# Joining each group's values burst with the next group's scores burst on TensorE, the values in an idle pair of PSUM banks

## Chip, cores and metric

One core of one Trainium2 chip. The metric is device time in microseconds of one execution: the median of three runs.

## What is computed

Local attention in chunks of 64 tokens, then a two-layer network with a squared ReLU. 8 sequences of 576 tokens with 8 heads of 64 give 4608 tokens of width 512; the hidden width is 2048. All data are float32.

```python
scores = scale * np.matmul(q_c, k_c.transpose(0, 1, 2, 4, 3))
scores = scores - np.max(scores, axis=-1, keepdims=True)
attn = np.exp(scores)
attn = attn / (np.sum(attn, axis=-1, keepdims=True) + 1e-09)
out = np.matmul(attn, v_c)
...
h = x @ w_in
r = np.maximum(h, 0.0)
g = s * (r * r) + b
return (g @ w_out).astype(np.float32)
```

## The kernel before

**Tiling.** The tokens come in 36 tiles of 128. The first four (class First) are done in a plain way while the weights are converted and written back to DRAM in pieces (kept). The other 32 tiles make four blocks of 8 tiles, 1024 tokens each, numbered 1 to 4; block 1 is the class Second, blocks 2 to 4 are the class Block. Every float32 product is made of three float32r products: an operand is split into a high part (hi, made on ACT) and a low rest (lo, made on DVE), and high x high, high x low and low x high are summed in PSUM.

**A block's products.** Blocks use a seven-product scheme for a 2x2 matrix product (P1, P7, P6, P2, P5, P4, P3, in this order, the list SEQUENCE). Layer one ("up") has four chains pp = 0 to 3 of seven products, slots 0 to 27 of a block. Layer two ("down") is one chain whose seven products take four slots each, slots 28 to 55. One slot is one product: 12 wide matmuls (128x128 weights, 512 columns), L575 for up, L624 for down (these lines are of the kernel before; the changed one has them a line further down). The names p0 to p55 in the code are these slots. Block 1 has a slightly different start and therefore 57 slots.

**PSUM.** Eight banks in four pairs. One pair, the tile ps_a, belongs to attention (steady_bank, L423). The other three, ps_o (two of them) and ps, are a ring for the chains: a Chain takes the ring's order and reverses it for the next chain, P1, P7 and P2 each begin one of the three pairs, and the other four products add onto these (Chain.bank, L443). On the way ACT copies a pair out (keep, L448) and DVE forms a quarter of the result from a pair and a copy (add, L455: form11 and others in up, end00 and others in down). form12 (L593) and the last quarter are read by ACT.

**Attention of the next block.** While a block runs its products, the attention of the block after it is done in four groups of two token tiles. One group's steps: load_qk and load_v (SP queue); scores (L318: 32 products 64x64x64 on TensorE, each two matmul records, into ps_a); peak and sub on DVE, which read ps_a; exp on ACT; sum, norm (add, reciprocal, multiply) and turn (transposing 32x32 blocks, L368) on DVE; swap, eight transfers of 64 KB that complete the transpose from SBUF to SBUF (L377, SP queue); values (L384, 32 products into ps_a again); x_out on ACT (L418), which copies ps_a into the tile xf. From xf, POOL makes sums and differences (x_sums, L506), ACT the high parts (xh, L524) and DVE the low ones (xl, L530).

**What sets the order.** Nothing is scheduled by the machine: each block has a list self.pre[slot] of named steps to be issued before a slot's product, filled by plan_up, plan_down and plan_following, and the engines take their instructions in that order. `self.at(slot, ...)` appends to a slot's list; `self.pre[n + k][:0] = ...` puts steps at its front. In blocks 2 and 3 the scores of the four groups are issued in slots 3, 14, 25, 36 and their values in slots 13, 24, 35, 45 (GROUPS and END, L481). For block 1 and the part before it, a list written out by hand (ORDER, L26) replaces the plan; its names are "1:p45" for slot 45 of block 1, "2:values.3" for the values of group 3 of block 2. A second list, SLOTS (L91), says which of 45 SBUF places each new tile gets.

The weights of each product come from DRAM (stream, L545: tile st, six buffers, 512 KB each), issued on the SP queue five slots ahead. SP also carries the swaps and the loads and stores, in program order; an instruction that waits there holds what is behind it.

These steps come up below. gh and gl are the high part (L598, ACT) and the low part (L603, DVE) of the operand that one down product needs for one pp; they are issued four slots or more ahead of it. end00 (DVE, L456) reads the pair that P2, slots 40 to 43, has completed. less21 and t2 (L611) are subtractions on POOL in blocks 2 to 4.

Of the kernel before, what the change touches and what calls it, by code (L numbers as in the profile page):

```python
# [32 lines left out]
shift4 2:load_qk.0 more3 exp.0 load_v.3 more2 lo2 down0 relu2 sign4 sign3.1 copy2 add4 relu3 sum.0 down1 scale5 rest2
norm.0 hi3.0 add3.1 load6 hi4 up4 hi3.1 load7 tail5 keep0 lo3.0 transposes.0 shift5 copies.0 more4 lo4 copy3 values.0
relu4 sign5 down2 copy4 lo3.1 add5 tail6 rest3 rest4 scale6 up5 x_hi.0 shift6 load8 x_out.0 sign6 more5 scale7 x_lo.0
add6 down3 relu5 shift7 hi5 copy5 load9 scores.1 hi6 lo5 load_qk.2 tail7 up6 sign7 tail8 rest5 add7 more6 peak.1
scale8 up7 relu6 sub.1 load10 scale9 lo6 more7 keep1 hi7 down4 shift8 keep6 shift9 relu7 sign8 copy7 sign9 copy6 add8
down5 exp.1 rest6 rest7 scale10 sum.1 up9 lo7 hi8 load12 keep7 up8 tail10 norm.1 tail9 lo8 more9 add9 more8 down6
relu8 copy8 relu9 load11 rest8 keep3 shift10 transposes.1 copy9 sign10 down7 scale12 2:load_v.0 rest9 hi9 add10
copies.1 lo9 up10 tail12 load14 hi10 keep2 values.1 scale11 lo10 more10 x_hi.1 shift11 up11 sign11 tail11 x_lo.1  # L40
relu10 add11 more11 shift12 down8 x_out.1 relu11 load13 sign12 keep8 hi11 scores.2 copy11 add12 copy10 rest11 down9
peak.2 sub.2 load15 keep4 lo11 up13 exp.2 load_qk.3 scale14 rest10 sum.2 keep9 more13 hi12 up12 norm.2 scale13 tail14
keep5 more12 lo12 tail13 transposes.2 shift14 keep11 relu13 down10 shift13 sign13 copies.2 relu12 add13 values.2
copy12 rest12 down11 sign14 hi13 copy13 lo13 keep13 add14 x_hi.2 up15 rest13 scale15 keep10 x_lo.2 tail15 keep12 up14
shift15 hi14 more14 x_out.2 lo14 more15 relu14 sign15 scores.3 copy14 add15 relu15 rest14 down12 peak.3 copy15 sub.3
stream hi15 down13 rest15 exp.3 lo15 1:st9 1:st4 sum.3 keep14 down14 1:combine0.2 keep15 norm.3 1:combined_hi0.2
down15 1:combine0.3 last out0 transposes.3 1:combine0.5 copies.3 steady 1:p0 1:x_sums.0 1:combined_hi0.5
1:combined_hi0.3 1:keep_combined0.5.0 1:keep_combined0.2.0 values.3 2:load_v.1 1:combine0.6 1:p1 1:keep_combined0.3.0
1:combine0.4 1:combined_hi0.6 1:xh6.0 1:p2 x_hi.3 1:combined_lo0.3 1:relu11.0 x_lo.3 1:keep_combined0.3.1 1:p3
1:combined_lo0.2 x_out.3 1:combined_lo0.5 1:keep_combined0.2.1 out1 1:combined_hi0.4 1:x_sums.1 1:keep_combined0.5.1  # L50
2:scores.0 1:keep_combined0.6.0 1:xh2.1 1:p4 1:xh4.0 1:xh3.1 2:peak.0 1:relu21.0 2:sub.0 1:p5 1:combined_lo0.4 1:xh6.1
1:st5 1:xl2.1 1:keep_combined0.4.0 1:combine0.7 1:keep_combined0.4.1 1:p6 1:relu12.0 1:st7 1:combine1.0 1:xh4.1 1:p8
1:xh3.0 2:exp.0 1:xl6.0 1:combined_hi0.7 1:xl3.0 2:sum.0 1:p7 1:st6 1:keep0.1 1:xl3.1 1:st11 2:norm.0 1:p9 1:st8
1:relu22.0 1:combined_lo0.6 2:load_qk.1 1:xl6.1 1:xh2.0 2:turn.0 1:p11 1:keep3.1 1:xl2.0 2:swap.0.1 1:gh0.0 1:xl4.1
1:keep_combined0.7.0 1:combined_lo0.7 2:swap.0.3 1:p10 2:swap.0.7 1:combine1.1 2:swap.0.4 1:st13 2:swap.0.2 1:st14
1:p13 2:swap.0.0 1:keep2.1 1:xl4.0 2:swap.0.6 1:form11.1 1:combined_hi1.0 1:st12 2:swap.0.5 1:combine1.2
1:keep_combined0.6.1 1:p12 1:st10 1:keep_combined0.7.1 1:combined_hi1.2 1:form21.1 1:combined_hi1.1 1:p15 1:st17
1:combine1.3 1:square11.1 1:keep_combined1.2.0 1:combined_hi1.3 2:values.0 1:combined_lo1.1 1:st16 1:form22.1 1:p16
1:keep_combined1.1.1 2:x_out.0 1:combine1.4 1:p14 1:st18 1:keep3.2 1:keep_combined1.3.0 1:combined_lo1.2
1:combined_hi1.4 1:combine1.5 1:keep0.2 2:scores.1 1:st15 1:form12.1 1:p17 2:peak.1 1:combined_lo1.0 1:combine1.6  # L60
1:p18 1:keep_combined1.0.1 1:keep2.2 1:st22 1:keep_combined1.2.1 1:square22.1 1:keep_combined1.0.0 2:sub.1 1:p20
1:st20 1:form11.2 2:exp.1 1:square21.1 2:sum.1 1:p19 1:st19 1:combined_lo1.4 1:keep_combined1.1.0 1:combined_hi1.6
2:norm.1 1:combined_hi1.5 1:keep_combined1.6.0 1:p22 1:form22.2 2:turn.1 1:p21 1:form21.2 2:swap.1.6 1:st21 1:gl0.0
2:swap.1.1 1:square21.2 2:swap.1.0 1:p23 1:less11.0 2:swap.1.4 1:st25 1:keep0.3 1:combined_lo1.3 2:swap.1.5
1:keep_combined1.4.0 1:form12.2 1:combine1.7 2:swap.1.2 1:p24 1:st23 2:swap.1.3 1:gh0.1 2:swap.1.7 2:load_qk.2
1:keep3.3 1:gl0.1 1:p25 1:st24 1:keep2.3 1:less11.1 1:combined_hi1.7 1:st29 1:less12.1 1:square11.2 1:p26 1:st37
1:form11.3 1:gh3.1 1:t2.0 2:xh0.0 2:values.1 1:gl3.1 1:st26 1:gh1.0 1:keep_combined1.5.0 1:keep_combined1.3.1
1:less12.0 1:p27 2:x_out.1 1:square11.3 1:combined_lo1.5 1:form22.3 2:scores.2 1:st27 1:gh1.2 column_sums 1:gl1.0
1:p28 1:gh3.0 1:square22.2 1:combined_lo1.7 1:gl3.0 1:p29 1:st28 1:gh0.3 2:peak.2 2:xh1.0 1:combined_lo1.6 1:gh0.2
1:p30 1:gh5.0 1:form21.3 1:st30 1:keep_combined1.7.1 1:keep_combined1.5.1 1:gl0.2 1:keep_combined1.7.0  # L70
1:keep_combined1.4.1 1:t2.1 1:keep_combined1.6.1 1:p33 1:st33 2:sub.2 1:less11.2 2:exp.2 1:p34 1:form12.3 2:sum.2
2:norm.2 1:gh2.0 1:gh1.1 2:turn.2 1:square22.3 1:gl0.3 1:st31 1:st34 1:less12.2 biases 1:p31 1:p41 2:load_v.2
2:swap.2.3 1:gh3.2 1:less11.3 2:swap.2.5 1:gh4.1 2:swap.2.2 1:less12.3 1:p32 1:st32 1:gh2.1 1:gl3.2 2:swap.2.0 1:gh3.3
1:gl2.0 2:swap.2.1 1:gh4.3 1:p35 2:swap.2.7 1:gl1.2 1:keep0.down 2:swap.2.6 2:load_qk.3 1:gh5.1 1:gl2.1 2:swap.2.4
1:square21.3 1:p37 1:gl1.1 1:st38 2:st0 1:st39 1:gl3.3 1:t2.2 1:p38 1:st35 1:gl4.1 1:gh2.2 1:gh1.3 1:combine0.0 1:p36
1:st36 1:gh4.0 1:gl2.2 finish 1:t2.3 2:values.2 store 1:less21.1 1:p42 2:x_out.2 1:gl5.1 2:load_v.3 1:gh6.1 1:st40
1:combine0.1 2:xh0.1 1:gh2.3 2:scores.3 1:st42 2:xl0.1 1:p39 2:xl0.0 2:peak.3 1:gl2.3 1:p43 1:st41 2:sub.3 1:gl1.3
# [5 lines left out]
2:x_out.3 2:x_sums.1 1:combined_lo0.0 1:p51 1:st50 1:gl5.3 1:p52 1:st52 1:gl5.2 2:xh3.1 1:p53 1:st51
1:keep_combined0.0.1 1:end10 1:scaled10 2:x_sums.0 1:p54 2:xh2.1 2:xh6.1 1:scaled00 2:xl6.1 1:p55 2:st4 2:st1 2:xh3.0
2:xh2.0 2:xh4.0 1:p56 2:st2 2:xh5.1 2:xl4.0 1:scaled11 2:xl3.1 2:xl5.1 2:xh4.1 2:xl3.0 1:end01 2:st3 2:xl5.0 1:store10
2:xl2.0 3:load_v.0 2:xh6.0 2:xl1.1 2:xl1.0 1:store00 1:store11 2:xl2.1 2:xl6.0 2:xl4.1
"""

# [18 lines left out]
"""  # L107


@with_exitstack  # L110
def local_attention_then_squared_relu_mlp(ctx: ExitStack, tc, qkv, w, s, b, out):
# [10 lines left out]
    N = 2  # L122
# [959 lines left out]
```

## Time and profile before

| | |
|---|---|
| time, median of 3 runs | 775.91 us (775.17 to 779.9) |
| span of the profiled execution | 775.4 us; the page gives no other time of it |
| PE busy | 765.4 us, 99% of the span |
| DVE, ACT, POOL busy | 544.9, 489.4, 158.8 us |
| granted TensorE clock | full in all 40 slices |

How to read it: the span runs from the first to the last instruction of one execution. PE is TensorE's matmuls, PEld its weight loads, DVE is VectorE, ACT ScalarE, POOL GpSimd, SP the queue that issues transfers. L624 is line 624 of the kernel. A row of the timeline gives start (us from the span's start), duration, engine, line, operation, tiles out<-in, shapes, how many instructions were merged, and in brackets how long the engine was idle before and who released it. Matmul ends are modelled and the duration of one contains its passage through the array, so the steps between starts are what counts on PE. In block 2, slot 36 starts behind the scores burst at 399.06 us and slot 45 behind the values burst at 424.86 us.

### The profile page before, as it was taken

What the parts mean: (1) busy time and instruction counts of PE and PEld (TensorE: products, weight loads), DVE (VectorE), ACT (ScalarE), POOL (GpSimd) and SP (SyncE); (2) the same over time, 40 slices, a digit from 0 to 9 for tenths busy, and PEclk for the clock granted to TensorE, in tenths of its full rate; (3) what the DMA queues carried; (4) which work ended last, traced back from release to release, by engine and by line L of the source; (5) the groups of instructions that cost most, each with busy time, mean ns of one, the idle gap of its engine ahead of it and who ended that gap; (6) DMA issues with size and microseconds to landing.
All of it is one profiled execution on the core that took longest, in us unless ns stands there. A gap on an engine that the chain in (4) does not pass through costs nothing.

```text
span 775.4 us, 13741 instructions
## 1 busy us (share of the span) xinstructions
PE 765.4 (99%) x5526; PEld 629.5 (81%) x5526; DVE 544.9 (70%) x572; ACT 489.4 (63%) x585; POOL 158.8 (20%) x74
## 2 busy tenths in 40 slices
PE   8999999999999999999999999999999999999997
PEld 7788788888888888888888888888888888888886
DVE  6987889999999945563769746555698723365742
ACT  5998796757976545566662656667454656674451
POOL 2544340000000060000337300004175001022500
PEclk9999999999999999999999999999999999999999
DMA  9999999899999889768485787767657765555563
GB/s 339 347 345 327 319 363 367 279 343 358 350 307 350 281 300 330 252 229 279 163 294 171 272 289 236 278 206 258 226 215 260 242 227 199 196 194 194 191 216 109
DMA packets 86738, 207.47 MB, mean 268 GB/s; under 512 B 8084, under 2 KB 37524, under 8 KB 86676
## 3 DMA queue, kind: packets, MB, share of 16 engines
q1 hardware_dynamic: 86528, 206.47, 77.0%
q8 instruction: 44, 0.72, 0.4%
q14 instruction: 18, 0.15, 0.1%
q10 hardware_dynamic: 148, 0.13, 0.1%
HBM read 160.96 MB, written 39.32 MB: 258 GB/s over the span
## 4 chain that ended last, share of the span: by engine, by line
PE 93%; DMA 4%; ACT 2%; DVE 1%; issue 0%; SPq 0%; DVEq 0%; ACTq 0%
PE ps_o L624 24%; PE ps_o L575 23%; PE ps L624 14%; PE ps L575 12%; PE ps_h L905 5%; PE ps_o L930 5%; PE ps_a L384 2%; PE ps_a L318 2%; PE ps L840 1%; PE ps_o L840 1%; DMA raw<-in_w_dram 1%; DMA kept<-wh 1%; PE ps_o L639 1%; PE ps L639 1%; DMA pT<-pB 1%; DMA qk<-in_qkv_dram 1%
## 5 line engine op out<-in xcount | busy, mean ns | idle before, releaser
L603 DVE TENSOR_TENSOR gl<-q,gh 128x1024 fp32r<-128x1024 f32 x112 | 156.6, 1425 | 45.8 <-ACT gh L598 45.6
L575 PE MATMUL ps_o<-xh,st 128*128 128x512 f32 x552 | 177.6, 391 | 0.0
L624 PE MATMUL ps_o<-gh,st 128*128 128x512 f32 x544 | 171.8, 391 | 0.0
L611 POOL TENSOR_TENSOR q<-q 128x1024 f32<-128x1024 f32 x24 | 66.7, 2784 | 325.1 <-PE ps L575 131.3
L598 ACT CAST gh<-q 128x1024 fp32r<-128x1024 f32 x112 | 113.2, 1047 | 22.5 <-DVE q L611 21.9
L575 PEld LDWEIGHTS ps_o<-xh,st 128*128 128x128 f32 x552 | 103.6, 188 | 22.3
L624 PEld LDWEIGHTS ps_o<-gh,st 128*128 128x128 f32 x544 | 102.1, 188 | 21.8 <-DMA st<-kept 0.4
L575 PE MATMUL ps_o<-xl,st 128*128 128x512 f32 x276 | 107.5, 389 | 0.0
L624 PE MATMUL ps_o<-gl,st 128*128 128x512 f32 x272 | 105.9, 389 | 0.0
L624 PE MATMUL ps<-gh,st 128*128 128x512 f32 x320 | 101.5, 391 | 0.0
L575 PE MATMUL ps<-xh,st 128*128 128x512 f32 x288 | 95.3, 392 | 0.0
L624 PEld LDWEIGHTS ps<-gh,st 128*128 128x128 f32 x320 | 60.1, 188 | 12.6
L581 ACT ACTIVATE q<-q 128x1024 f32<-128x1024 f32 x45 | 47.4, 1054 | 33.6 <-DVE q L456 33.6
L456 DVE TENSOR_TENSOR q<-ps_o,tmp 128x1024 f32<-128x1024 f32 x30 | 36.7, 1222 | 45.3 <-PE ps_o L575 44.4
L450 ACT COPY tmp<-ps_o 128x1024 f32<-128x1024 f32 x40 | 40.5, 1011 | 40.7 <-PE ps_o L575 24.1
L575 PEld LDWEIGHTS ps<-xh,st 128*128 128x128 f32 x288 | 54.0, 188 | 12.0
L624 PE MATMUL ps<-gl,st 128*128 128x512 f32 x160 | 62.3, 389 | 0.0
L575 PEld LDWEIGHTS ps_o<-xl,st 128*128 128x128 f32 x276 | 51.8, 188 | 10.4
L611 DVE TENSOR_TENSOR q<-q 128x1024 f32<-128x1024 f32 x40 | 50.6, 1269 | 13.4 <-ACT q L594 12.6
L624 PEld LDWEIGHTS ps_o<-gl,st 128*128 128x128 f32 x272 | 51.1, 188 | 10.5
L506 POOL TENSOR_TENSOR xt<-xf 128x512 f32<-128x512 f32 x12 | 23.0, 1913 | 177.3 <-ACT xf L418 177.3
L881 ACT ACTIVATE o<-o,bias,sb 128x512 f32<-128x512 f32 x28 | 21.2, 808 | 59.4 <-DVE o L456 59.4
(116 smaller groups left out, 1193.9 us busy)
## 6 DMA issues: line engine op xcount, KB each, us to landing
st<-kept SPq DMA_DIRECT2D x221, 512.0 KB, 4.4
qk<-in_qkv_dram SPq DMA_DIRECT2D x36, 512.0 KB, 5.3
raw<-in_w_dram SPq DMA_DIRECT2D x32, 512.0 KB, 7.0
v<-in_qkv_dram SPq DMA_DIRECT2D x36, 256.0 KB, 6.4
kept<-wh SPq DMA_DIRECT2D x18, 512.0 KB, 6.8
out_dram<-o SPq DMA_DIRECT2D x17, 512.0 KB, 6.6
kept<-f SPq DMA_DIRECT2D x16, 512.0 KB, 7.0
pT<-pB SPq DMA_DIRECT2D x96, 64.0 KB, 3.1
```

The costliest lines, as they stand in the source:

```text
L450: nc.scalar.copy(out=self.u[product], in_=self.bank_of(product))
L456: nc.vector.tensor_tensor(out=to, in0=self.ps[bank], in1=self.u[kept], op=ALU.add)
L506: engine.tensor_tensor(out=to, in0=x, in1=y, op=ALU.subtract)
L575: nc.tensor.matmul(out=to[:, k], lhsT=a[:, cols], rhs=x[:, c, :], start=i in BEGINS and c == 0 and n == 0, stop=c == 1 and n == 2, skip_gr ...
L581: nc.scalar.activation(out=q, in_=q, func=AF.Relu)
L598: nc.scalar.copy(out=self.g[i, pp][0], in_=self.q[quarter, pp])
L603: nc.vector.tensor_tensor(out=lo, in0=self.q[quarter, pp], in1=hi.bitcast(F32), op=ALU.subtract)
L611: engine.tensor_tensor(out=self.q[to, pp], in0=self.q[x, pp], in1=self.q[y, pp], op=ALU.subtract)
L624: nc.tensor.matmul(out=self.to[i][:, d], lhsT=a[:, cols], rhs=x[:, k, :], start=i in BEGINS and pp == 0 and k == 0 and n == 0, stop=pp == ...
L881: nc.scalar.activation(out=to[:, d], in_=source[:, d], func=AF.Identity, scale=s_col, bias=bias[:, d0 + d:d0 + d + 1])
L905: nc.tensor.matmul(out=self.h[j][:, cols], lhsT=w[c][low], rhs=x[:, c, :], start=low + c + i == 0, stop=low == 1 and c == NHP - 1)
L930: nc.tensor.matmul(out=self.acc[d], lhsT=a, rhs=x, start=(j == 0 and i == 0), stop=(j == NJ - 1 and i == 2))
```

## The change

The steps of a group are taken apart into those from its scores on and those from its values on. A list BURSTS holds four slots of a block; in each, the values of group m and the scores of group m + 1 are issued one directly behind the other. In the last of them the scores are those of group 0 of the block after the next. Values then go to a pair of the ring that is idle (IDLE: the chain and which of its three pairs), scores stay in ps_a. x_out follows a slot later. Further: end00 is put at the front of slot 44's list, where it stood behind that slot's gh and gl; norm and turn go to the end of their slot's list, where they stood at its front. For block 1 only the end of the hand-written list changes, where its last values (2:values.3) are now followed by 3:scores.0. The scores of group 0 of a block, which were issued in that block's own predecessor at slot 3, are now issued at slot 45 of the block before that one. SLOTS is new from block 1's middle on.

```diff
 ORDER = """
...
-3:load_qk.0 1:gl6.3 1:keep_combined0.1.1 1:end00 2:values.3 1:st49 1:end11 1:keep_combined0.0.0 1:p50 1:gl6.2
...
+1:gl5.0 1:p49 1:st48 1:gl6.3 1:keep_combined0.1.1 1:end00 2:values.3 3:scores.0 1:st49 1:end11 1:keep_combined0.0.0
...
         def values(self, apart=False):
-            tiles = [self.bank(2) for _ in range(N if apart else 1)]
+            tiles = [self.values_bank() if self.values_bank else self.bank(2) for _ in range(N if apart else 1)]
...
     class Block:
-        UP, TILES, ORDER, GROUPS, LEAD, END = 28, 56, (0, 2, 1, 3), (3, 14, 25, 36), 5, 9
+        BURSTS, IDLE = (15, 26, 36, 45), ((1, 0), (3, 2), ("down", 2), ("down", 2))
+        UP, TILES, ORDER, LEAD = 28, 56, (0, 2, 1, 3), 5
...
+        def idle(self, chain, pair):
+
+            return pick(self.chains[chain].order[pair])
...
-            at(16, *self.ends(0, 0))
+            end, scaled = self.ends(0, 0)
+            self.pre[u + 16].insert(0, end)
+            at(16, scaled)
...
-        def plan_attention(self, n, a, last, following):
-            def names(*steps):
-                m = following.groups.index(a)
...
-            self.at(max(n - self.LEAD, 0), *names("load_qk", "load_v"))
-            end = ((self.END, "values"), (self.END + 1, "x_out")) if last else ((10, "values", "x_out"),)
-            for k, *steps in ((0, "scores"), (1, "peak", "sub"), (2, "exp"), (3, "sum"), (4, "norm", "turn"),
-                              (5 if last else 6, "swap"), *end):
-                self.pre[n + k][:0] = names(*steps)
+        def plan_scores(self, at, block, m, swap):
+            self.at(max(at - self.LEAD, 0), *block.steps(m, "load_qk", "load_v"))
+            for k, *names in ((0, "scores"), (1, "peak", "sub"), (2, "exp"), (3, "sum"), (4, "norm", "turn"),
+                              (swap, "swap")):
+                where = len(self.pre[at + k]) if names[0] == "norm" else 0
+                self.pre[at + k][where:where] = block.steps(m, *names)
 
         def plan_following(self, following):
-            for n, a in zip(self.GROUPS, following.groups):
-                self.plan_attention(n, a, a is following.groups[-1], following)
-            z = self.GROUPS[-1] + self.END - 4
+            following.register()
+            after = following.following
+            for m, (at, idle) in enumerate(zip(self.BURSTS, self.IDLE)):
+                if m < 3:
+                    self.plan_scores(at, following, m + 1, 5 if m == 2 else 6)
+                elif after:
+                    self.plan_scores(at, after, 0, 9)
+                if idle:
+                    following.groups[m].values_bank = later(self.idle, *idle)
+                self.pre[at][:0] = following.steps(m, "values")
+                self.pre[at + 1][:0] = following.steps(m, "x_out")
+            z = self.BURSTS[-1] - 4
...
     class Second(Block):
-        UP, TILES, ORDER, GROUPS, LEAD, END = 8 * CLASSIC + 7 * (NPP - CLASSIC), 4 * CLASSIC + 7 * (NPP - CLASSIC) + 28, (0, 1, 2, 3), (4, 17, 28, 39), 7, 10
+        BURSTS, IDLE = (14, 27, 38, 45), (None, None, None, ("down", 2))
+        UP, TILES, ORDER, LEAD = 8 * CLASSIC + 7 * (NPP - CLASSIC), 4 * CLASSIC + 7 * (NPP - CLASSIC) + 28, (0, 1, 2, 3), 7
```

Three places show the order. The first is PE in block 2 around slot 45: the last wide matmul of slot 44, the values of group 3 (ps_a or ps<-pT,v), and the first of slot 45. In square brackets stand the semaphores that a row waits for. Before:

```order
L624 MATMUL ps_o<-gh,st 128x512
L384 MATMUL ps_a<-pT,v 64x64 [waits DMAHW5_49,DMAHW4_49,DMAHW6_49,DMAHW3_49,PE_49]
L384 MATMUL ps_a<-pT,v 64x64
L384 MATMUL ps_a<-pT,v 64x64 [waits DMAHW2_49,DMAHW7_49,DMAHW1_49,DMAHW0_49]
L384 MATMUL ps_a<-pT,v 64x64 x29
L624 MATMUL ps_o<-gh,st 128x512 [waits Activation_49]
L624 MATMUL ps_o<-gl,st 128x512 [waits DVE_49]
```

The same place now:

```order
L625 MATMUL ps_o<-gh,st 128x512
L384 MATMUL ps<-pT,v 64x64 [waits DMAHW2_49,DMAHW1_49,DMAHW7_49,DMAHW0_49,DVE_49]
L384 MATMUL ps<-pT,v 64x64
L384 MATMUL ps<-pT,v 64x64 [waits DMAHW5_49,DMAHW6_49,DMAHW4_49,DMAHW3_49]
L384 MATMUL ps<-pT,v 64x64 x29
L318 MATMUL ps_a<-qk 64x64 x32
L625 MATMUL ps_o<-gh,st 128x512 [waits Activation_49]
```

The scores of the next block's group 0 have come in behind the values, and the values wait for DVE, which reads the pair ps in end00.

The second place is DVE in block 2, slots 39 to 44: sum (z<-p), the low parts of P2 and P5 (gl), norm (three rows on z and p), turn (pB<-p), the first xl of the next block, and end00 (o<-ps,tmp). Before:

```order
L339 TENSOR_REDUCE z<-p 128x16
L603 TENSOR_TENSOR gl<-q,gh 128x1024
L346 TENSOR_SCALAR z<-z 128x16
L347 RECIPROCAL z<-z 128x16
L350 TENSOR_TENSOR p<-p,z 128x1024
L368 STREAM_TRANSPOSE pB<-p 128x1024
L603 TENSOR_TENSOR gl<-q,gh 128x1024 x4
L530 TENSOR_TENSOR xl<-xf,xh 128x2x256
L603 TENSOR_TENSOR gl<-q,gh 128x1024
L456 TENSOR_TENSOR o<-ps,tmp 128x1024
```

The same place now:

```order
L339 TENSOR_REDUCE z<-p 128x16
L604 TENSOR_TENSOR gl<-q,gh 128x1024 x2
L346 TENSOR_SCALAR z<-z 128x16
L347 RECIPROCAL z<-z 128x16
L350 TENSOR_TENSOR p<-p,z 128x1024
L368 STREAM_TRANSPOSE pB<-p 128x1024
L604 TENSOR_TENSOR gl<-q,gh 128x1024 x3
L531 TENSOR_TENSOR xl<-xf,xh 128x2x256
L456 TENSOR_TENSOR o<-ps,tmp 128x1024
L604 TENSOR_TENSOR gl<-q,gh 128x1024
```

One gl has moved ahead of norm, and end00 ahead of one gl.

The third place is ACT in block 2, up to slot 38: high parts (gh), copies of a pair (tmp), x_out of group 2 (xf) and exp of group 3 (p). Before:

```order
L598 CAST gh<-q 128x1024 x3
L450 COPY tmp<-ps_o 128x1024
L598 CAST gh<-q 128x1024 x2
L418 COPY xf<-ps_a 128x2x4x64 x2
L598 CAST gh<-q 128x1024 x2
L450 COPY tmp<-ps_o 128x1024
L598 CAST gh<-q 128x1024
L335 ACTIVATE p<-p 128x1024
```

The same place now:

```order
L599 CAST gh<-q 128x1024 x3
L450 COPY tmp<-ps_o 128x1024
L599 CAST gh<-q 128x1024 x4
L450 COPY tmp<-ps_o 128x1024
L418 COPY xf<-ps 128x2x4x64 x2
L599 CAST gh<-q 128x1024
L335 ACTIVATE p<-p 128x1024
```

x_out has moved behind two more gh and a copy.

## Rows read from the trace of the kernel before

**Rows 1.** The page: span, and part 1, busy us, share, instructions.
```profile
span 775.4 us, 13741 instructions
PE 765.4 (99%) x5526; PEld 629.5 (81%) x5526; DVE 544.9 (70%) x572; ACT 489.4 (63%) x585; POOL 158.8 (20%) x74
```

**Rows 2.** The chain that ended last, in order of time: start us, us, what.
```profile
411.33 10.88 PE ps L624 x48
```

**Rows 3.** Timeline of PE, block 2: start us, us, engine, line, operation, count.
```profile
394.70 0.39 PE L624 MATMUL ps_o<-gh,st 128*128 128x512 f32 x1
395.02 1.16 PE L384 MATMUL ps_a<-pT,v 64*64 64x64 f32 x64
396.12 0.50 PE L624 MATMUL ps_o<-gh,st 128*128 128x512 f32 x1
396.45 0.39 PE L624 MATMUL ps_o<-gl,st 128*128 128x512 f32 x1
...
399.06 1.16 PE L318 MATMUL ps_a<-qk 64*64 64x64 f32 x64
...
424.86 1.16 PE L384 MATMUL ps_a<-pT,v 64*64 64x64 f32 x64
```

**Rows 4.** Instructions of line L384: duration ns min/median/max, first and last start us.
```profile
L384 PE MATMUL ps_a<-pT,v x1024: 218/218/267, 44.7 to 588.7; 64*64 64x64 f32 x171
```

**Rows 5.** Timeline of DVE, block 2, slots 35 to 45.
```profile
398.36 2.36 DVE L603 TENSOR_TENSOR gl<-q,gh 128x1024 fp32r<-128x1024 f32 x2 [3.87 <-ACT gh L598]
400.64 1.22 DVE L326 TENSOR_REDUCE m<-ps_a 128x16 f32<-128x1024 f32 x1
...
416.42 7.88 DVE L603 TENSOR_TENSOR gl<-q,gh 128x1024 fp32r<-128x1024 f32 x4
...
424.83 1.21 DVE L603 TENSOR_TENSOR gl<-q,gh 128x1024 fp32r<-128x1024 f32 x1
425.96 1.21 DVE L456 TENSOR_TENSOR o<-ps,tmp 128x1024 f32<-128x1024 f32 x1
```

**Rows 6.** Timeline of ACT, block 2, slot 35.
```profile
396.31 1.07 ACT L418 COPY xf<-ps_a 128x512 f32<-128x512 f32 x2 [3.74 <-PE ps_a L384]
```

**Rows 7.** Timeline of POOL, block 2, the first of four sums of x.
```profile
414.10 2.28 POOL L506 TENSOR_TENSOR xt<-xf 128x512 f32<-128x512 f32 x1
```

**Rows 8.** Timelines of PE and DVE, block 3, slot 45.
```profile
587.80 1.16 PE L384 MATMUL ps_a<-pT,v 64*64 64x64 f32 x64
588.91 1.21 DVE L456 TENSOR_TENSOR o<-ps_o,tmp 128x1024 f32<-128x1024 f32 x1
```

**Rows 9.** Timelines of DVE and PE, end of block 1.
```profile
270.71 1.22 DVE L456 TENSOR_TENSOR o<-ps_o,tmp 128x1024 f32<-128x1024 f32 x1
272.81 1.16 PE L384 MATMUL ps_a<-pT,v 64*64 64x64 f32 x64
```

**Rows 10.** Timelines of PE, ACT and DVE, block 2, slots 14 and 25.
```profile
333.92 1.16 PE L318 MATMUL ps_a<-qk 64*64 64x64 f32 x64
335.08 1.01 ACT L593 ACTIVATE q<-ps 128x1024 f32<-128x1024 f32 x1
335.15 1.22 DVE L326 TENSOR_REDUCE m<-ps_a 128x16 f32<-128x1024 f32 x1 [0.76 <-PE ps_a L318]
...
366.67 1.22 DVE L456 TENSOR_TENSOR q<-ps_o,tmp 128x1024 f32<-128x1024 f32 x1 [7.64 <-PE ps_o L575]
```

**Rows 11.** SP's timeline; transfers by line from 414 us on and on the page (to landing).
```profile
416.52 4.95 SPq L377 DMA_DIRECT2D pT<-pB  x8
...
pT<-pB SPq DMA_DIRECT2D x8, 64.0 KB, 2.0
...
st<-kept SPq DMA_DIRECT2D x221, 512.0 KB, 4.4
```

**Rows 12.** Busy time in a stretch: sum, PE, PEld, DVE, ACT, POOL, clock, DMA.
```profile
425.00:450.00 25.00, 25.00 (x170) 20.82 (x169) 19.68 (x18) 15.32 (x22) 7.54 (x4) 1.00 0.81 280
```

More of the change, by code (lines that the diff above doesn't have):

```diff
@@ L33 @@
[L33 to L77, printed above, removed]
@@ L83 @@
[L83 to L86, printed above, removed]
+sub.b shift0.1 transposes.a exp.b sign0.1 busy3 copies.a sum.b add0.1 values.a scale1 invert.b load2 hi0.1 busy4 scale.b
@@ new lines @@
+more15 relu14 sign15 scores.3 copy14 add15 relu15 rest14 down12 peak.3 copy15 sub.3 stream hi15 down13 rest15 exp.3 lo15
+1:st9 1:st4 sum.3 keep14 down14 1:combine0.2 keep15 norm.3 1:combined_hi0.2 down15 1:combine0.3 last out0 transposes.3
+1:combine0.5 copies.3 steady 1:p0 1:x_sums.0 1:combined_hi0.5 1:combined_hi0.3 1:keep_combined0.5.0 1:keep_combined0.2.0
+values.3 2:load_v.1 1:combine0.6 1:p1 1:keep_combined0.3.0 1:combine0.4 1:combined_hi0.6 1:xh6.0 1:p2 x_hi.3
+1:combined_lo0.3 1:relu11.0 x_lo.3 1:keep_combined0.3.1 1:p3 1:combined_lo0.2 x_out.3 1:combined_lo0.5
@@ new lines @@
+1:combine0.0 1:p36 1:st36 1:gh4.0 1:gl2.2 finish 1:t2.3 2:values.2 store 1:less21.1 1:p42 2:x_out.2 1:gl5.1 2:load_v.3
+1:gh6.1 1:st40 1:combine0.1 2:xh0.1 1:gh2.3 2:scores.3 1:st42 2:xl0.1 1:p39 2:xl0.0 2:peak.3 1:gl2.3 1:p43 1:st41
+2:sub.3 1:gl1.3 2:exp.3 1:gh5.2 1:p40 2:sum.3 1:st43 1:keep3.down 1:gl4.0 1:combined_hi0.1 2:norm.3 1:p44 1:keep2.down
+1:st44 1:combined_hi0.0 2:turn.3 2:xh5.0 2:xh1.1 1:less21.2 1:p45 2:swap.3.5 2:swap.3.2 1:combined_lo0.1 1:gh6.2
+2:swap.3.0 1:keep_combined0.1.0 1:gh4.2 1:gl4.3 2:swap.3.4 1:p46 3:load_qk.0 1:st45 1:gl4.2 2:swap.3.1 2:swap.3.7
@@ L754, in plan_following, with steps, register @@
-        def plan_following(self, following):
-            for n, a in zip(self.GROUPS, following.groups):
-                self.plan_attention(n, a, a is following.groups[-1], following)
-            z = self.GROUPS[-1] + self.END - 4
+        def steps(self, m, *names):
+            if names == ("swap",):
+                return [f"{self.n}:swap.{m}.{k}" for k in range(8)]
+            return [f"{self.n}:{name}.{m}" for name in names]
+        def register(self):
+            for m, a in enumerate(self.groups):
+                for name in ("load_qk", "load_v", "scores", "peak", "sub", "exp", "sum", "norm", "turn", "values", "x_out"):
+                    self.op(f"{name}.{m}", getattr(a, name))
+                for k in range(8):
+                    self.op(f"swap.{m}.{k}", a.swap, k)
@@ L949, in local_attention_then_squared_relu_mlp @@
     for block, following in zip(blocks, blocks[1:] + [None]):
-        block.plan(following)
+        block.following = following
+    for block in blocks:
+        block.plan()
     coming = blocks[0].groups
```

67 lines of the change are left out of this document (51 added, 16 removed), and 20 rows, old and new, of the table SLOTS.

## The prediction

> **What bounds the kernel now.** I read the page first. TensorE (PE) is busy for 765.4 of the span's 775.4 us [rows 1], so nothing else can be worth much unless it makes PE wait or shortens what PE does. Next came PE in order of time. The wide matmuls follow each other every 0.227 us (48 of them take 10.88) [rows 2], so one slot of 12 lasts 2.72 us. Attention interrupts this stream with bursts of 64 short matmuls on 64x64 quarters, and that is the place to look: what does one burst cost? The last wide matmul before a burst starts at 394.70, the second one behind it at 396.45 [rows 3]. Those 1.75 us hold two ordinary steps, 0.45, so a burst costs 1.30. Inside it the 64 records last 1.16 in all and the last of them 0.218 [rows 3, 4], so from the first start to the last it takes 0.94, or 15 ns each. The other 0.36 is entering and leaving: 0.32 from the last wide matmul to the burst, where 0.23 is usual, and a late, slow first wide matmul behind it.
>
> **What the change takes away.** Where values and scores stand together, the second burst is entered from the first. The pair should cost 1.30 + 64 x 0.015 = 2.26 instead of 2.60, which is 0.34 less. The order shows eight such pairs: one at the end of block 1, four in block 2, three in block 3 (the last values of block 3 have no scores behind them). 8 x 0.34 = 2.7 us. No row of before shows a join, so the bounds are 0 (a join costs as much as leaving and entering) and 2.7. I take 2.7, since the values and scores bursts have the same shapes and prices in the rows and the first scores behind a join have at most one wait, on a load issued five slots before.
>
> [...]
>
> **What it adds: values wait for whoever read the idle banks last.** Before, values and scores shared one pair of banks of their own (ps_a). Now values go where a chain product was. Each of the eight places has its last reader:
> - Slot 15: form12 on ACT reads the bank in slot 14. Before, it ran at 335.08, 1.0 us long, right after its scores burst at 333.92 and before its slot was over [rows 10]. The values burst is a slot of 2.72 later. Cover: 1.4 us or more. Cost 0.
> - Slot 26: form11 on DVE, which at 366.67 had been idle for 7.64 us waiting for PE [rows 10]; it takes 1.22 of the 2.72. Cost 0.
> - Slot 36: the bank has been unused since slot 28. Cost 0.
> - Slot 45, and the end of block 1: end00 on DVE reads the bank that the product of slot 43 finished, so it has one slot, and DVE is the engine with a backlog. In block 1, end00 ran 270.71 to 271.93, and its values started at 272.81 [rows 9]: 0.88 us in hand, cost 0. In block 2, end00 ran 425.96 to 427.17, while values started at 424.86 [rows 3, 5]. That didn't matter before, as nobody on PE waited for it. Now PE does.
>
> How late will end00 be in block 2? Two things move it forward. First, it was put ahead of one gl, which ran 424.83 to 426.04 [rows 5]; taking that start, end00 ends at 424.83 + 1.21 = 426.04. Second, the run of DVE work that leads to it began with peak at 400.64, held up by two gl from 398.36 on [rows 5]; their gh on ACT stood behind x_out, which had waited 3.74 us for the values of slot 35 [rows 6]. Now two more gh stand ahead of x_out, so peak should begin 1.23 after its burst starts, as elsewhere (335.15 after 333.92) [rows 10]: 399.06 + 1.23 = 400.29, 0.35 earlier. From there DVE has nearly no gap, so end00 ends at about 425.7. The way on PE from the scores of slot 36 to the values of slot 45 is unchanged (nine slots), so values are due at 424.86 and wait 0.85, with the restart 0.9. Block 3 repeats it (end00 at 588.91, values at 587.80: 1.11 apart, 1.10 in block 2) [rows 8]. Two waits of 0.9 are 1.8 us. Bounds for one: 0, and 427.17 - 424.86 = 2.3 if end00 gains nothing.
>
> Why DVE is late there: a gl takes 1.21 alone (424.83), but the four from 416.42 on took 7.88, 1.97 each, while POOL ran the sums of x from 414.10 on [rows 5, 7]. Without that, end00 would end 7.88 - 4 x 1.21 = 3.0 earlier and nobody would wait. [...]
>
> **The steps that only move.** Of group 0 everything moves from the next block's first slots into the last slots of this one. DVE gets seven instructions there, five about as long as peak's 1.22 [rows 5] and two short ones, some 6.3 us as an estimate, on top of 19.68 of 25 us [rows 12]; the excess of about 1 us spills into the next block's first slots, which lose the same 6.3 us of work. I take 0; if the excess holds PE, it costs up to that 1 us in two blocks, 2 us. On SP the eight transfers of a turned block occupy the queue for 4.95 us [rows 11], and the weight loads stand behind them. A weight load goes out five slots (13.6 us) ahead and lands after 4.4 [rows 11], so 9 us are in hand: cost 0. norm and turn now stand behind the other work of their slot: one gl (1.2 to 2.0) in slot 40, two subtractions in slot 30. In block 2 the last of the transfers for slot 45 was issued by 421.47 and lands 2.0 after its issue [rows 11], so before 423.5, with 424.86 the due time; 1.4 in hand take up most of that delay, and what is left stays behind end00. Cost 0.
>
> **Sum.** -2.7 + 1.8 = -0.9. The page gives the profiled execution's span, 775.4, and no other time of it: 774.5. The median of the runs, 775.91, is 0.5 above that span, so I forecast 775.0.
>
> **Rivals.**
> - A, no wait: gh and gl of slot 36 run earlier, so POOL's subtractions do too, the two engines meet less, and end00 is done by 424.86. It needs 0.85 us more than I gave it; one or two gl at 1.21 instead of 1.97 do that. Against it: the sums of x are still there from 414.10 on [rows 7], and they alone stretch four gl. Time 775.9 - 2.7 = 773.2.
> - B, slower: end00 gains nothing. The moved gl lets POOL take one more turn before norm and each DVE operation behind pays for it, so end00 ends at 427.17 as before. Place: values of slot 45 in blocks 2 and 3. Price 2.3 each, 4.6 together; from 1.35 each on it eats all of the 2.7. Time 775.9 - 2.7 + 4.6 = 777.8.
> - C, the change doesn't do what it says: the joined bursts still pay 0.34 between them, and the waits of 0.9 remain. Time 775.9 + 1.8 = 777.7.
>
> **How the numbers follow.** Forecast 0.45, A 0.33, B 0.15, C 0.05, something unseen 0.02. The forecast's own range is 774.2 to 776 (waits of 0.5 to 1.3). For 8 in 10 the range goes from A to B: 773.0 to 777.8. A measurement of this kernel can tell about 1%, 7.8 us, from no change. All cases lie inside that: within 1% 0.97, faster 0.01, slower 0.02.
>
> **What would show it.** Right: in the profile after, PE in order of time shows 128 short matmuls in one piece of about 2.1 us, and the wide stream resumes 2.26 later than it would have; PE's waits show two of about 0.9 for DVE o, before the values of slot 45 in blocks 2 and 3, and none at the other six pairs. Wrong: no such wait (A), waits over 1.35 (B), a gap inside the joined bursts (C), or waits of PE for pT, xf, xl or st, which I put at 0.

## The result and the profile after

The changed kernel is slower: 782.44 us median of 6 runs (781.06 to 783.83) beside 775.76 for the kernel before (6 runs). The ratio is 1.0078, 95% interval [1.0063, 1.0092]. I had forecast 775.0, with a range of 773.0 to 777.8: it is still within 1% of before, to which I gave 0.97, but outside the range. The profiled execution's span went from 775.4 [rows 1] to 780.7.

The page of the kernel after: span, busy times, one line of the DMA queues (packets, MB, share) and the shares of the chain that ended last.

```profile
span 780.7 us, 13757 instructions
PE 766.4 (98%) x5526; PEld 632.7 (81%) x5526; DVE 548.6 (70%) x572; ACT 489.6 (63%) x585; POOL 153.5 (20%) x74
...
q8 instruction: 44, 0.72, 0.3%
...
PE 91%; DVE 3%; DMA 2%; ACT 2%; issue 1%; SPq 0%; DVEq 0%
```

TensorE has the same 5526 matmuls, and its busy time grew by only 1.0 us. So PE stands still for longer, and the chain has 1% of "issue", time in which it waited for nothing that the profile shows. PE's waits say where:

```profile
PE ps_o L576 <- issue: 2.7, 1, 2.7
PE ps_o L625 <- issue: 2.1, 1, 2.1
...
PE ps_o L384 <- DVE o L456: 0.6, 1, 0.6
```

The third line is the wait for end00 that I had forecast. The first two are in no step of the prediction. Here they are in PE's timeline, block 2, slots 26 and 36 (start us, us, line, operation, count; in brackets the idle time before):

```profile
366.14 0.39 PE L576 MATMUL ps<-xh,st 128*128 128x512 f32 x1
366.46 1.16 PE L384 MATMUL ps_o<-pT,v 64*64 64x64 f32 x64
367.44 1.11 PE L318 MATMUL ps_a<-qk 64*64 64x64 f32 x64
371.26 0.50 PE L576 MATMUL ps_o<-xh,st 128*128 128x512 f32 x1 [2.71 <-issue]
...
400.30 1.16 PE L384 MATMUL ps<-pT,v 64*64 64x64 f32 x64
401.28 1.11 PE L318 MATMUL ps_a<-qk 64*64 64x64 f32 x64
402.32 0.50 PE L625 MATMUL ps_o<-gh,st 128*128 128x512 f32 x1
402.66 0.39 PE L625 MATMUL ps_o<-gl,st 128*128 128x512 f32 x1
405.18 0.62 PE L625 MATMUL ps_o<-gh,st 128*128 128x512 f32 x2 [2.13 <-issue]
```

The joins work: 64 values and 64 scores follow each other without a break, which [rows 3] show apart. But behind two of the eight joins PE stands idle for over 2 us. At slot 36 the gap comes two wide matmuls after the burst. In both gaps the next instruction is an ordinary wide matmul. What follows a gap is the second part of the price, seen in the busy time by stretch (columns as in [rows 12]):

```profile
366.00:368.60 2.60, 2.55 (x131) 2.06 (x129) 1.55 (x2) 2.57 (x4) 2.30 (x2) 1.00 1.04 425
368.60:371.30 2.70, 0.04 (x1) 0.04 (x1) 2.67 (x3) 2.67 (x5) 0.40 (x1) 1.00 0.64 237
...
372.00:374.90 2.90, 2.90 (x8) 2.22 (x8) 0.47 (x1) 2.10 (x3) 0.00 (x0) 0.50 0.03 7
374.90:377.90 3.00, 3.00 (x14) 2.45 (x13) 2.00 (x2) 0.00 (x0) 0.00 (x0) 0.92 0.29 78
...
406.00:409.20 3.20, 3.20 (x10) 2.48 (x9) 2.27 (x2) 2.87 (x4) 2.38 (x1) 0.51 0.46 183
```

The granted clock, 1.00 in [rows 12], is 0.50 from 372.00 to 374.90 and 0.51 from 406.00 to 409.20; by the trace's clock records it is at half for 3.41 us after each gap. Seven or eight wide matmuls then start 0.427 us apart instead of 0.227. That costs 1.6 us after either gap, summed over their steps.

At slot 45 of block 3 end00 decides, as forecast, with 0.58 where I said 0.85. DVE first, then PE; [rows 8] are those of before:

```profile
591.10 0.68 DVE L531 TENSOR_TENSOR xl<-xf,xh 128x512 fp32r<-128x512 f32 x1
591.70 1.21 DVE L456 TENSOR_TENSOR o<-ps_o,tmp 128x1024 f32<-128x1024 f32 x1
```

```profile
592.96 1.37 PE L384 MATMUL ps_o<-pT,v 64*64 64x64 f32 x64 [0.58 <-DVE o L456]
```

In block 2 nobody waits there, since the two gaps had delayed PE.

**Theory.** What does PE wait for when the profile shows nothing? The theory is: for its own instructions. The queue called "instruction" in the page brings 44 packets of 16,384 bytes. PE executes some 11,300 instructions by the trace, 257 for each packet; I take 256 to a packet (a segment), an estimate. In the quiet stream at the end, behind 622 us, a fetch starts every 250 to 269 instructions, 27 to 30 us apart. A burst of 64 short matmuls is 128 instructions (a weight load and a matmul each) and a semaphore instruction or two. A joined pair is 256: a whole segment in 1.9 us. And in both gaps a fetch is under way: it starts at 369.05 and at 402.90, 2.6 us after the burst began, and PE resumes 2.2 and 2.3 us after the fetch started. PE stopped at counts 6337 and 6849 of executed instructions, 512 apart: both 193 modulo 256. So: the pair eats up what has been fetched, and where it begins decides whether PE runs dry.

Rival: the gap belongs to these places (the idle bank's reader, a late transfer, a wait that the trace doesn't show) and would stay there wherever the stream's segments end. Second rival: dense short matmuls stop PE by themselves.

In before the queue brings 44 packets too, and none of PE's waits is put down to "issue"; here two are, each behind a join.

### The profile page after: what moved, and what is told of

Its sections match the earlier page's. It is cut to its first block, busy times and chain, and to the rows that moved or that the text cites. A ratio compares the mean times of both kernels' runs of the same rounds, so it can differ in the third digit from the quotient of the medians.

```text
span 780.7 us, 13757 instructions
## 1 busy us (share of the span) xinstructions
PE 766.4 (98%) x5526; PEld 632.7 (81%) x5526; DVE 548.6 (70%) x572; ACT 489.6 (63%) x585; POOL 153.5 (20%) x74
## 4 chain that ended last, share of the span: by engine, by line
PE 91%; DVE 3%; DMA 2%; ACT 2%; issue 1%; SPq 0%; DVEq 0%
PE ps_o L576 23%; PE ps_o L625 23%; PE ps L625 13%; PE ps L576 12%; PE ps_o L953 6%; PE ps_h L928 5%; PE ps_a L318 2%; PE ps L862 1%; PE ps_o L862 1%; DVE gl L604 1%; DMA kept<-wh 1%; PE ps_a L384 1%; PE ps_o L384 1%; PE ps_o L640 1%; PE ps L640 1%
## 5 line engine op out<-in xcount | busy, mean ns | idle before, releaser
L233 POOL TENSOR_TENSOR f<-f,raw 128x1024 int32<-128x1024 int32 (+1 forms) x18 | 43.0, 2389 | 67.0 <-DVE f L227 11.9
```

Of the source, the lines that this page charges most:

```text
L233: nc.gpsimd.tensor_tensor(out=i, in0=i, in1=low.bitcast(I32), op=ALU.add)
```

## Experiments

**1 to 4. The same kernel, moved along its segments.** A few small matmuls in the start-up, written to the tile that the start-up's own filler matmuls write (busy), shift everything behind them in PE's stream. No other instruction changes. 25 calls are 100 instructions:

```diff
+    def fill():
+        for k in range(25):
+            cols = slice(k % 2 * D, k % 2 * D + D)
+            nc.tensor.matmul(out=busy[cols, 0:D], lhsT=ones[0:D, 0:D], rhs=ones[0:D, 0:D], start=True, stop=True)
...
+    op("fill", fill)
...
-... sum.a busy2 tail0.1 ...
+... sum.a busy2 fill tail0.1 ...
```

*Kernel before, 25 calls* (b_shift100). 

> The kernel before with 25 more small matmuls (64x64 quarters of a tile of ones, 100 more instructions of TensorE) in a start-up stretch in which TensorE waits for data anyway; nothing else is touched. It is the control for the next three. Fetch theory: no burst of 64 short matmuls can run the instruction stream dry wherever it starts, so the time is that of before, 775.8 to 776.2, and TensorE has no new gap. Rival (places and waits): the same, 775.8. Rival (start-up itself matters): over 777.

*Changed kernel, 25 calls* (a_shift100). 

> The changed kernel with the same 100 instructions ahead. Every joined burst then starts elsewhere in the 256-instruction segments of TensorE's stream: counted as executed instructions modulo 256, the eight joins go from 141, 172, 194, 189, 161, 39, 61, 56 to 241, 16, 38, 33, 5, 139, 161, 156. Fetch theory: the two gaps of 2.7 and 2.1 us came since the bursts at 194 and 189 ate a whole segment in 1.9 us; none stands near 194 now, so both gaps go and with them the two falls of the granted clock (some 3.2 us): before's 775.8, less 2.9 of the joins, plus two waits for end00 of about 0.65 each, 774.2 (773.5 to 775). Rival (the gaps hang on these places: a bank's reader, a transfer, a wait): nothing there is touched, gaps and time stay, 782.4. Rival (density alone stops TensorE): gaps stay, 782.

*Changed kernel, 5 calls* (a_shift20). 

> The changed kernel with 5 small matmuls, 20 instructions, ahead. The joins start at 161, 192, 214, 209, 181, 59, 81, 76. Fetch theory in numbers: the gap is 2.71 us for a burst at 194 (where the next fetch is called for as the burst begins) and less by 0.113 us, half a wide matmul, for each instruction between, on either side. So in block 2: slot 15 now a gap of 2.5, slot 26 shrinks to 0.45, slot 36 to 1.0, slot 45 gets 1.2; time near 781 (779 to 783). If besides it takes a late wait ahead of the burst to hold the instruction queue back (as at slots 26 and 36), slot 15 and slot 45 get no gap or a small one, and the time is near 777. Rival (places): gaps of 2.7 and 2.1 at slots 26 and 36 as before, none at 15 and 45, 782.4.

*Changed kernel, 33 calls* (a_shift132). 

> The changed kernel with 33 small matmuls, 132 instructions, ahead. The joins start at 17 (end of block 1), in block 2 at 48, 70, 65, 37, in block 3 at 171, 193, 188. Fetch theory: block 2 has no gap, and block 3 gets one of about 2.6 us at slot 26 and one of about 2.0 at slot 36, each with a fall of the clock: 774.2 + 4.6 + 3.2 - 0.65 (the wait for end00 of block 3 is taken in by the gaps) = 781.4. Rival (places or waits of block 2): the gaps stay in block 2, none in block 3, 782.4.

Measured, ratio to before: control 1.0002 [0.9993, 1.0011]; shift by 100 0.9987 [0.9975, 0.9998]; by 20 1.0031 [1.0020, 1.0043]; by 132 1.0086 [1.0068, 1.0104]. The medians are 776.43, 775.11, 778.65 and 783.13 us, beside 776.34 for before in the same series. Shift 100 lies 0.1 above the range of its expectation. Shift 132 lies 1.7 above its 781.4: its second gap is 2.4 instead of 2.0, and in the profile only that one was followed by a fall of the clock. The waits of PE put down to "issue" in shift 20, then in shift 132:

```profile
PE ps_o L630 <- issue: 2.4, 1, 2.4
```

```profile
PE ps_o L581 <- issue: 2.7, 1, 2.7
PE ps L630 <- issue: 2.4, 1, 2.4
```

Shift 100 has none. In its timeline the wide stream follows slot 26's pair at once:

```profile
365.34 0.39 PE L581 MATMUL ps<-xh,st 128*128 128x512 f32 x1
365.66 1.16 PE L389 MATMUL ps_o<-pT,v 64*64 64x64 f32 x64
366.64 1.11 PE L323 MATMUL ps_a<-qk 64*64 64x64 f32 x64
367.69 0.50 PE L581 MATMUL ps_o<-xh,st 128*128 128x512 f32 x1
368.03 0.39 PE L581 MATMUL ps_o<-xl,st 128*128 128x512 f32 x1
```

From 365.34 to 368.03 are 2.69 us, less two steps of 0.227 is 2.24 for the pair. Every other join that has neither a gap nor a wait costs the same. Two single bursts cost 2.60 by the prediction's reading: 0.36 is saved per join, 0.34 was forecast.

Shift 132 moved the gaps to slots 26 and 36 of block 3, as its expectation said. So both rivals fall: the same instructions at the same places, as dense as ever, lose nothing or lose it elsewhere. The expectation for shift 20 is only half right. It has one gap, behind slot 45 (burst start at 179), and slots 15, 26 and 36, starting at 192, 214 and 209, have none. A formula by position alone is wrong. In those three the fetch had started 2.5 to 5.8 us ahead of the burst. Of the two versions in the expectation, the second (a late wait ahead of the burst is needed as well) fits slots 15, 26 and 36; it had not foreseen that slot 45, with its wait for end00, is such a place.

**5. Take the late wait away.** At slot 26 the bank's reader on DVE ends at 365.13, 1.3 us before the burst. At slot 36 the eight transfers of pT go out from 393.69 on for 4.96 us, and PE's queue stood at the values' last semaphore until 400.06, 0.24 us before the burst (start us, us, DVE, then SP):

```profile
363.90 1.23 DVE L456 TENSOR_TENSOR q<-ps_o,tmp 128x1024 f32<-128x1024 f32 x1 [6.33 <-PE ps_o L576]
```

```profile
393.69 4.96 SPq L377 DMA_DIRECT2D pT<-pB  x8
```

The theory adds, as a guess from these two places: PE's queue doesn't run ahead past a wait that isn't met, and so doesn't call for the instructions behind it. For group 2 alone, norm and turn go back to the front of their slot (a_norm2_front):

```diff
-                where = len(self.pre[at + k]) if names[0] == "norm" else 0
+                where = len(self.pre[at + k]) if names[0] == "norm" and m != 2 else 0
```

> The changed kernel with norm and turn of group 2 alone back at the front of their slot (two tile buffers trade places so that each keeps its lifetime); no instruction of TensorE moves, the joins start where they did in the changed kernel, 194 at slot 26 and 189 at slot 36. The transfers that the values of slot 36 wait for then go out some 7 us earlier, and TensorE's queue is not held at their semaphore right up to the burst. Fetch theory with the hold (a late wait keeps the queue from running ahead, so that the fetch is called for only inside the burst): the gap at slot 36 goes with its fall of the clock, the one at slot 26 stays at 2.7: about 778.5 (777.5 to 779.5). Fetch theory by position alone: both gaps stay, 782.4. Rival (a late transfer itself is the gap): slot 36's gap goes too, and so would the gap in the kernels with a shift; those have none although their transfers were not moved.

The transfers now go out from 387.68 on. PE's waits:

```profile
PE ps_o L576 <- issue: 2.7, 1, 2.7
...
PE ps_o L625 <- issue: 0.8, 2, 0.4
```

Slot 26, left alone, keeps its 2.7. At slot 36, with the same start at 189, the idle time falls from 2.13 to 0.39: the fetch starts 0.67 us after the burst's start instead of 2.60. The second 0.4 is new, behind slot 45, whose values now start 0.15 late, behind end00. The ratio is 1.0059 [1.0043, 1.0074], 780.57 us, 2 more than expected. The profiled execution took 778.56 at a mean granted clock of 1.000; the two runs over 781 have 0.996 and 0.997, as the runs of the changed kernel have (0.995 to 0.998). So some executions of this kernel had falls of the clock that the profiled one didn't have.

All gaps behind bursts in one table, from the records of the instruction queue. "Start" is the burst's, in executed instructions modulo 256:

```
kernel, place                      start  fetch after burst start   PE resumes after fetch
after, block 2 slot 26              194     2.59                      2.21
after, block 2 slot 36              189     2.60                      2.28
shift 20, block 2 slot 45           179     4.10                      2.18
shift 132, block 3 slot 26          193     2.46                      2.30
shift 132, block 3 slot 36          188     3.21                      2.21
norm2 front, block 2 slot 26        194     2.48                      2.32
norm2 front, block 2 slot 36        189     0.67                      2.47
norm2 front, block 2 slot 45        159     4.17                      2.34
shift 80, end of block 1            221     2.39                      2.49
shift 80 late xl, end of block 1    221     2.29                      2.51
scores later, block 2 slot 36        85    -0.77                      2.30  (scores alone)
no gap: after, slot 15              172    -0.04
no gap: shift 20, slots 15, 26, 36  192, 214, 209   -2.51, -2.76, -5.79
no gap: shift 100, block 3 slot 26  161     2.36 (31 instructions left behind the burst)
```

The rows of shift 80 and scores later belong to experiments below. PE resumes 2.2 to 2.5 us after its fetch starts, eleven times out of eleven, and each time it had stopped at count 193 or 194 modulo 256, by the theory the end of a segment. What changes is when the fetch starts and how many instructions are left behind the pair by then.

In all eleven the fetch starts 2.8 to 4.0 us after PE's queue passed the values' last semaphore. The semaphore instructions of slot 36's values, durations in ns (shortest/median/longest) and starts in us, in the changed kernel and with norm in front:

```profile
L384 PEldq EVENT_SEMAPHORE  x4: 51/51/1261, 396.9 to 398.8; - x4
```

```profile
L384 PEldq EVENT_SEMAPHORE  x4: 51/51/51, 394.6 to 395.6; - x4
```

The last one ends at 400.06 in the changed kernel, and the fetch came at 402.90; with norm in front it ends at 395.70, 3.1 us before the burst, and the fetch came at 399.46. That fits the hold, which this one experiment moved; at slots 26 and 45 it is read from the traces and not tried.

What fills these 3 to 4 us isn't shown. The fetch is itself a DMA transfer (queue q8 of the page), and from the burst to the fetch the DMA share of the profile is 0.91 to 1.08 (1 is all 16 busy) in the ten cases where the fetch comes behind the burst. No run takes this traffic away, so it stays a rival for part of the delay. Alone it doesn't explain slot 36: in the 3 us ahead of the burst it was 0.52 in the changed kernel and no fetch came, and 0.95 with norm in front, where the fetch came 1.9 us sooner. Something moves the fetch without any burst, too: 10 us and more behind the last one it starts anywhere from count 152 to 202 over the 13 profiles, 50 instructions or 5.7 us of the wide stream.

**6. Undo the join, keep the idle banks.** Scores go one slot behind the values in blocks 2 and 3 (a_scores_later):

```diff
-            for k, *names in ((0, "scores"), (1, "peak", "sub"), (2, "exp"), (3, "sum"), (4, "norm", "turn"),
-                              (swap, "swap")):
+            for k, *names in ((1, "scores", "peak", "sub"), (2, "exp"), (3, "sum"), (4, "norm", "turn"), (swap, "swap")):
```

> The changed kernel with the scores of blocks 2 and 3 one slot behind the values, so that 12 wide matmuls stand between the two bursts (seven joins undone, the one at the end of block 1 stays); values still go to the idle banks, everything else stands where it was. Fetch theory: 129 instructions, then 24 in 2.7 us, then 129: the fetch has time, no gap of 2 us or more; a rest of up to 1.5 us may be left at slot 26, where the first burst still starts at 194. Time 775.8 - 0.36 (one join) + two waits for end00 of 0.65 each = 776.7, up to 779 with a rest. Rival (the idle banks, their readers or their order make the gaps): the gaps stay ahead of the same instructions, 782 or, without the joins' 2.5 us, 785.

1.0149 [1.0134, 1.0165], 788.14 us: the time was a clear miss. The gaps of 2.7 and 2.1 are gone (one of 0.5 is left, inside the scores of slot 36), as the fetch theory had it. But PE's waits show a new bound:

```profile
PE ps_o L384 <- DVE o L456: 3.3, 1, 3.3
PE ps L384 <- DVE o L456: 3.3, 1, 3.3
```

Scores a slot of 2.72 later start DVE's run of slots 36 to 45 later too. Its peak begins 4.2 us later behind the values of slot 36 than in shift 100: the slot, the join undone, and 1.1 us lost inside the two bursts. That run has next to no idle time in it, so end00 came 4.2 us later as well. The two waits are 2.7 longer each than in shift 100; seven joins cost 2.5; and the granted clock fell again around the end of each wait (0.54 from 427 to 430 us, 0.50 from 595 to 601). I had moved a step and not counted who stands behind it. The place is the one that rival B named. Its cause, turns taken by POOL (in before two gl beside its subtractions, at 405.18 and 409.03, took 2.79 and 2.56 us instead of 1.21), isn't seen to grow: from peak to the end of end00 the run lasts 25.2 us in both kernels.

**7 and 8. Two more positions.** 46 calls (a_shift184), and no call at all but 18 fewer of the start-up matmuls, `enumerate((5, 3, 5, 1, 1, 1))` for `(8, 6, 12, 2, 4, 2)` (a_fewer_starts), which is the same position modulo 256.

> The changed kernel with 46 small matmuls, 184 instructions, ahead, so that no joined burst starts between 122 and 223 of a segment: 69, 100, 122, 117, 89 up to block 2, 223, 245, 240 in block 3 (with the shift by 100 two of them started at 156 and 161, and the next fetch came with some 26 instructions left). Fetch theory: no gap and no fall of the clock in any run, 0.2 to 0.4 us more of start-up than with 25 matmuls; ratio to before 0.997 to 0.999, 774 to 775.3, and fewer of the runs near 778 that the shift by 100 had. If the block-3 bursts at 223 to 245 are on the wrong side (the fetch called for ahead of the burst is still too late), a gap shows at slot 15 of block 3 and the time is 777 or more. Rival (places): 782.4.

> The changed kernel with 18 fewer of the 34 start-up matmuls on a tile of ones (72 fewer instructions of TensorE), nothing added. 72 fewer and 184 more are the same position modulo 256, so the joins start at 69, 100, 122, 117, 89, 223, 245, 240 again. Fetch theory: no gap behind any join, 774 to 775.3, if the start-up itself, where TensorE then has less to do while it waits for data, doesn't get longer; that may cost or give up to 1 us. Rival (places): 782.4. Rival (the added matmuls did something else than shift): gaps at slots 26 and 36, 782.

1.0012 [1.0004, 1.0021] and 0.9997 [0.9988, 1.0007], 777.19 and 775.78 us, both above the 774 to 775.3 expected; no gap behind a join in either. (The first has one of 0.3 us in the start-up, ahead of a filler matmul, at count 194 again; PE resumes 2.3 us after the fetch.) Their spans, 775.8 and 774.5, differ from shift 100's 772.6 ahead of the first join alone: it starts at 274.52, 273.18 and 271.34, and from there to the end it is 501.3 us in all three. In before and its control it is 502.6 (from 272.81 and 272.90). So without gaps the change is worth 1.3 us from the first join on. The start-up differs by more, up to 3.2 us, and not in the order of the number of calls (the longest has 46, the next 18 matmuls fewer, the shortest 25); why wasn't tried. It hides the gain in the medians: 1.2 us less than before, 1.2 more and 0.3 less. That the gaps went because of something else that the added calls do is refuted: removing matmuls cured them as well.

**9 to 11. A version that beats both.** What is left of the price is end00. Just ahead of it on DVE stands an xl of 0.68 us, which nobody needs soon. In blocks 2 and 3 it goes behind end00 (late_xl; a few tile buffers trade places):

```diff
-                self.at(z + 2 + k, *following.x_split(0, i))
+                hi, lo = following.x_split(0, i)
+                self.at(z + 2 + k, hi)
+                self.at(z + 2 + k + (k == 0), lo)
```

> The changed kernel with 20 small matmuls, 80 instructions, ahead, the control of the next one. The joins start at 221, 252, 18, 13, 241, 119, 141, 136 of a segment, none between 142 and 220. Fetch theory: no gap behind a join; from the end of block 1 on the time is that of the kernels shifted by 100 and 184 and of the one with fewer start-up matmuls, 501.3 us from the first join's start to the end of the span; ratio to before 0.997 to 1.000, by how long the start-up takes. Rival (places): 782.4.

> The kernel with 80 instructions ahead, and in blocks 2 and 3 one xl subtraction on DVE (0.68 us) that stood ahead of end00 now stands behind end00 and the gl after it (three or four tile buffers trade places so that each keeps its lifetime). The values of slot 45 wait 0.6 us for end00 in both blocks without this. Theory: DVE is the bound of that stretch alone, so end00 ends 0.68 earlier, both waits go (to 0.1 at most), 1.2 to 1.3 us less than the control, 500.0 us from the first join on. Rival (end00 is held by something that moves with it, a subtraction beside POOL or the bank): waits of 0.4 or more stay, and nothing is gained.

> The same edit to xl with the shift by 100, the kernel that was fastest so far (0.9987 of before). Theory: 1.2 us less, 0.997 of before (0.9955 to 0.9985), no gap behind a join, no wait for end00 over 0.1. Rival: 0.9985 or more, waits stay.

With the shift by 100: 0.9972 [0.9961, 0.9983], 774.53 us, the lowest median of all; the interval overlaps that of shift 100 without it. DVE and PE at slot 45 of block 2:

```profile
421.96 1.21 DVE L461 TENSOR_TENSOR o<-ps,tmp 128x1024 f32<-128x1024 f32 x1
423.09 1.21 DVE L609 TENSOR_TENSOR gl<-q,gh 128x1024 fp32r<-128x1024 f32 x1
424.22 0.68 DVE L536 TENSOR_TENSOR xl<-xf,xh 128x512 fp32r<-128x512 f32 x1
```

```profile
422.82 0.39 PE L630 MATMUL ps_o<-gh,st 128*128 128x512 f32 x1
423.22 1.31 PE L389 MATMUL ps<-pT,v 64*64 64x64 f32 x62
```

The step into the burst is 0.40 here and 1.00 in shift 100 (421.53 to 422.53). The same in block 3 makes it 500.1 us from the first join on, 1.2 less, as expected.

The shift by 80 missed: 1.0039 [1.0027, 1.0051], and 1.0028 [1.0016, 1.0039] with the late xl. Behind the join at the end of block 1, at 221, a start that I had called safe:

```profile
PE ps_a L323 <- issue: 2.9, 1, 2.9
```

The fetch started 2.39 after the burst there, while a burst at 223 (shift 184, block 3, slot 15) had its fetch more than 4 us ahead. What differs is a late wait: in shift 80 PE's queue stood at a semaphore of the values from 268.96 to 271.11, 0.8 us before the burst at 271.96; at slot 15 of shift 184 no semaphore instruction stands in the 4.9 us before. So an unsafe start can lie past 194 too, and where the limit is wasn't found.

## Why the prediction was wrong

**The step that failed** is the price of a burst: "The pair should cost 1.30 + 64 x 0.015 = 2.26". The pair itself costs that (2.24). But the step took for granted that PE's next instruction is always there. It is the only term of the sum that counts instructions, and it counted their time alone. 256 of them in 1.9 us are as many as one fetch brings by that estimate, against 2.2 to 2.5 us from a fetch's start to PE's resuming. The first gap is 2.93 from start to start where 0.15 is usual behind a pair, the second 2.52 where a wide step is 0.23: 2.78 and 2.29. With the slow clock behind them, 1.6 twice, that is 8.3 us. None of the rivals had it; "something unseen" had 0.02.

By the time from the first join to the end: 501.3 without gaps + 8.3 - 0.7 (end00 no longer waited for in block 2) = 508.9. Measured: 780.7 - 272.11 = 508.6, which is 6.0 more than before's 502.6. The spans differ by 5.3, since the profiled execution reached the first join 0.7 us earlier than before's. The medians differ by 6.7, since the execution of before that was profiled was slow by 1.4: in every run that has both, the time is 1.7 to 1.9 above the span, so its 775.4 stands for some 777.2 and not for the median of 775.76. The forecast's step of 0.5 from span to median rests on that slow execution; it does no harm, since the forecast is the median less 0.9 either way.

**Joins, 2.7 us:** right. 0.36 each, 2.9 in all.

**Values wait for end00, 0.9 each in blocks 2 and 3:** right in place and kind, 0.7 instead of 0.9 with the restart (1.00 less the usual 0.32), shown in the kernels without a gap. The forecast of these two together, 0.9 gained, stands beside 1.3 gained from the first join on. So the forecast was right for the part it saw.

**Slots 15, 26 and 36, cost 0:** nobody waits for these banks, as said. But at slot 26 the reader ended 1.3 us ahead of the burst, and I asked only whether PE waits. By the theory it holds the queue back all the same: PE's queue passed the values' semaphores at 365.34, and the fetch started 3.7 us later.

**norm and turn behind the other work, "Cost 0":** I worked out slot 45 and not slot 36. There the transfers landed 0.24 us before they were due. No wait, but the fetch started late; with the step put back the idle time fell from 2.13 to 0.39.

**DVE's spill and SP's queue, 0:** no wait of PE shows them in the kernels without a gap. Moved by one slot more (experiment 6) DVE's backlog alone cost two waits of 3.3.

## What to carry to other kernels

Count the instructions of a dense stretch, not only their time: where an engine executes as many as one fetch brings within two or three microseconds (here 256 in 1.9), look in the trace for "issue" waits of over 2 us that begin behind it, and at the instruction queue's transfers beside them. Here such a gap depended on where the stretch falls in the stream (shifted by 0, 20, 100 and 132 instructions, the kernel had two gaps, one, none and two at other places), so a harmless change far ahead can switch it on or off, and a change of order should be timed at two or three shifts before it is judged. A semaphore met just in time can be paid for by what stands dense behind it, though PE shows no wait for it: at slot 36 the idle time was 2.13 us where the last one was met 0.24 us before the burst, and 0.39 where it was met 3.1 us before.

## What the runs showed of the hardware that I had not expected

PE ran dry after 427 to 509 instructions from the start of the fetch before (507 at slot 26 of the changed kernel): no more than two segments were ahead of it. The transfer itself takes 0.9 to 1.0 us of the 2.2 to 2.5.

The half clock follows some gaps and not others. In the profiles it came after both gaps of the changed kernel, after the second of shift 132 and after that of shift 80 (five to eight wide matmuls at 0.427, 1.5 to 1.7 us lost each time), and after that of shift 80 with the late xl, where it lasted twice as long (mean granted clock of the profiled execution 0.996, beside 0.998 in shift 80). It didn't come after the first of shift 132, the 2.4 us of shift 20 or the 2.7 at slot 26 with norm in front, where the granted clock stayed at 1.00. The place alone doesn't decide: of the ten runs of shift 20, five have a mean granted clock of 1.000 and five 0.998. What tells them apart wasn't tried.
